# A linear-attention and SoLU kernel with the hidden features laid out eight to a partition: row-contiguous w_out, a permuting w_in cast, masks built first

## The chip, the cores and the metric

The kernel runs on one NeuronCore of a Trainium2 chip, in one launch. The metric is device time in microseconds (us). The kernel before was run ten times; the median is 157.78 us and the runs lie between 152.22 and 159.04 us. One further view comes from a profiled execution, whose own time is 158.03 us and whose span, from the first to the last instruction, is 156.3 us.

## What is computed

Two stages follow each other. The first is a linear attention with a decaying state per head (4 batches, 8 heads, 768 steps, head size 48):

```
for t in range(S):
    cur = einsum('bhd,bhe->bhde', u * k_t, v_t)
    y_t = einsum('bhd,bhde->bhe', r_t, state + cur)
    state = w_t[..., None] * state + einsum('bhd,bhe->bhde', k_t, v_t)
```

The result is seen as a matrix x of 3072 tokens by 384 features and goes through a feed-forward layer with 1024 hidden features:

```
h = x @ w_in                        # 384 -> 1024
solu = h * softmax(h)
ln = (solu - mean) / sqrt(var + 1e-6) * g_ln
out = ln @ w_out                    # 1024 -> 384
```

The sums over the 1024 hidden features (softmax, mean, variance, the last product) do not depend on the order in which the features are numbered, as long as w_in's columns, g_ln and w_out's rows use the same order.

## The kernel before

**Units.** The work is cut into 24 units: 6 chunks of 128 time steps by 4 batches. Each unit loads its k, r, w and v by four DMAs (192 KB each, in runs of one head of 48 floats, 192 bytes), all issued from SyncE's queue (SP). For each unit ScalarE takes the logarithm of w (`lw`), TensorE sums it along time (`cum`), ScalarE exponentiates (`exp`), VectorE scales k and r (`kp`), TensorE transposes them (`kt`, with `ident`), multiplies them to scores (`M`), applies them (`Y`), updates the state (`S`), and transposes the result (`X`). Then follow the hidden layer (`H`, 24 matmuls against `win_sb`), its exponential on ScalarE (`e`), the product (`he`) and the square (`hq`), the output product (`Oa`, `Ob`, against `w2`), the normalisation (`sq`, `qm`, `lv`), the scaled copy `o`, and the store `sto`.

**Order.** The order of all steps is written out by hand in the string `ORDER` (lines 24 to 54). A word names a stage, a unit and sometimes an engine (a for ScalarE, v for VectorE, g for GpSimd): `win2a` is the cast of slice 2 of w_in on ScalarE. The class `InOrder` (lines 57 to 75) chains the instructions that are made through `pe`, `act`, `dve`, `pool` and `sp`, so that each engine and the SP queue keep that order. Instructions made through `nc.gpsimd` or `nc.vector` directly, such as the memsets at the start, stand outside of the chain. The profile gives most instructions the line of `InOrder` (L71, or L68 for the first on an engine), so they are told apart by the names of their tiles.

**Weights.** The order on SP is: loads of units 0 to 2 with `small` (u and g_ln) among them, then `ldwin2`, `ldwin1`, `ldv1`, `ldwin0`, `ldwout0`, `ldwout1`, and the further loads. `ldwin` brings one slice of 128 rows of w_in (512 KB, 128 runs of 4 KB). `ldwout` brings four of the eight 128-row blocks of w_out (768 KB, 512 runs of 1.5 KB): hidden feature f sits on partition f % 128, block f // 128. The steps on the loaded weights are:

- `setup_rows` (line 200): TensorE spreads u over the partitions, then transposes the 8 x 128 tile `g_rows` into PSUM (`gt_ps`) with the 8 x 8 identity `ident_f`. `setup_rows_copy` (line 207): VectorE copies u to `u_bc` and makes the row scale `gr` from `gt_ps`.
- `setup_w_in` (line 222): ScalarE casts each slice of w_in to bf16, `win_f` to `win_sb`, three instructions.
- `setup_gain` (line 226): eight instructions `gw` scale w_out's blocks by `gr`; four run on ScalarE, two on VectorE, two on GpSimd. Blocks 0 to 3 come from the first half, 4 to 7 from the second.
- `setup_mean`, `setup_mean_copy`, `setup_w2` (lines 232 to 242): TensorE makes the column means from all eight `gw`, ScalarE copies them, and GpSimd adds them to each block, giving `w2`.

On ScalarE the order is `win2a win1a vb1a win0a gw1a gw0a e0 gw5a gw7a e1 lw3`. On TensorE it is `X1 H0 H1` and later `mean`; `H0` needs all three slices of `win_sb`.

**Masks.** `uti_neg`, `uts` and `ident` are 128 x 128 bf16 constants made on GpSimd (lines 153 to 162), and `ident_f` is made at line 192. `make_identity` is a library helper (a memset and an affine select, shown as masks.py in the profile).

Of the kernel before, what the change touches and what calls it, by code (L numbers as in the profile page):

```python
# [9 lines left out]
F32 = mybir.dt.float32  # L10
# [7 lines left out]
ALU = mybir.AluOpType  # L18
MULT, ADD = ALU.mult, ALU.add
# [59 lines left out]
def kernel(  # L79
# [12 lines left out]
    nc = tc.nc  # L92
    B, H, S, D = r.shape
    C = 128
# [5 lines left out]
    KF = DF // 128  # L100
    RDF = float(DF) ** 0.5
# [3 lines left out]
    pe, act, dve, pool, sp = (InOrder(tc, e) for e in (nc.tensor, nc.scalar, nc.vector, nc.gpsimd, nc.sync))  # L105
# [3 lines left out]
    consts = ctx.enter_context(tc.tile_pool(name="consts", bufs=1))  # L109
# [3 lines left out]
    small = ctx.enter_context(tc.tile_pool(name="small", bufs=4, space=bass.MemoryType.PSUM))  # L113

    live = [dict() for _ in units]
# [16 lines left out]


    u_row = consts.tile([1, DM], F32)
    g_rows = consts.tile([KF, 128], F32)
    win_f = consts.tile([128, KM, DF], F32)
    win_v = moe_w_in.rearrange("(ko ki) f -> ki ko f", ki=128)
    wout_f = consts.tile([128, KF, DM], F32)
    wout_v = moe_w_out.rearrange("(ko ki) d -> ki ko d", ki=128)

    def load_small():
        sp.dma_start(out=u_row, in_=u.rearrange("(o h) d -> o (h d)", o=1))
        sp.dma_start(out=g_rows, in_=moe_g_ln.rearrange("(ko ki) -> ko ki", ki=128))

    def load_w_in(j):
        sp.dma_start(out=win_f[:, j, :], in_=win_v[:, j, :])
# [1 line left out]
    def load_w_out(half):  # L148
# [2 lines left out]


    uti_neg = consts.tile([C, C], BF16)
    nc.gpsimd.memset(uti_neg, -1.0)
    nc.gpsimd.affine_select(out=uti_neg, in_=uti_neg, compare_op=ALU.is_ge, fill=0.0, base=0,
                            pattern=[[1, C]], channel_multiplier=-1)
    uts = consts.tile([C, C], BF16)
    nc.gpsimd.memset(uts, 1.0)
    nc.gpsimd.affine_select(out=uts, in_=uts, compare_op=ALU.is_gt, fill=0.0, base=0,
                            pattern=[[1, C]], channel_multiplier=-1)  # L160
    ident = consts.tile([C, C], BF16)
    make_identity(nc, ident)
    one_col = consts.tile([C, 1], BF16)
    nc.vector.memset(one_col, 1.0)
    own = consts.tile([C, HP, 2], F32)
# [18 lines left out]
    win_sb = consts.tile([128, KM, DF], BF16)  # L184
# [3 lines left out]
    nc.vector.memset(mean_w, -1.0 / DF)  # L188
    nc.vector.memset(w2[:, :, DM:], 1.0 / RDF)

    ident_f = consts.tile([KF, KF], F32)
    make_identity(nc, ident_f)
    ones_row = consts.tile([1, C], F32)
    nc.vector.memset(ones_row, 1.0)
    u_bc = consts.tile([C, H, D], BF16)
    gr = consts.tile([128, KF], F32)
# [3 lines left out]
    def setup_rows():  # L200
        u_ps = small.tile([C, DM], F32, tag="s", name="u_ps")
        pe.matmul(u_ps, lhsT=ones_row, rhs=u_row, start=True, stop=True)
        g_ps = small.tile([128, KF], F32, tag="s", name="gt_ps")
        pe.transpose(g_ps, g_rows, ident_f)
        live[0]["u_ps"], live[0]["g_ps"] = u_ps, g_ps

    def setup_rows_copy():
        dve.tensor_copy(out=u_bc.rearrange("t h d -> t (h d)"), in_=live[0]["u_ps"])
        dve.tensor_scalar(out=gr, in0=live[0]["g_ps"], scalar1=RDF, scalar2=None, op0=MULT)

    def copy(engine, out, in_):
        if engine is act:
            act.copy(out=out, in_=in_)
        else:
            engine.tensor_copy(out=out, in_=in_)
# [4 lines left out]
        pe.matmul(w_ps, lhsT=uti_neg, rhs=warm, start=True, stop=True)  # L220

    def setup_w_in(j, engine):
        copy(engine, win_sb[:, j, :], win_f[:, j, :])


    def setup_gain(f, engine):
# [359 lines left out]
    def part(stage, j):  # L586
# [5 lines left out]
        m=scores_copy, sel=scores_mask, Y=attend, y=y_copy, X=x_transposed, xT=x_copy, S=state, st=state_update,  # L592
        H=hidden, e=hidden_exp, he=hidden_mul, hq=hidden_square, Oa=part(output, 0), Ob=part(output, 1), sq=sums, qm=centre,
        lv=scale, o=scaled_out, sto=store, Oc=part(output, 2), oz=lambda i, engine: scaled_out(i, engine, 1),
        stz=lambda i: store(i, 1), sd=state_old, sa=state_add, win=setup_w_in, gw=setup_gain, wt=setup_w2, dm=warm_up,
        ldw=load("w", w), ldk=load("k", k), ldr=load("r", r), ldv=load("v", v), ldwin=load_w_in, ldwout=load_w_out,
    )
    once = dict(small=load_small, rows=setup_rows, ubc=setup_rows_copy, mean=setup_mean, mean_sb=setup_mean_copy)
    engines = dict(a=act, v=dve, g=pool)
    for word in ORDER.split():  # L600
        name, i, choice = re.fullmatch(r"([A-Za-z_]+)(\d*):?([a-z]?)", word).groups()
# [38 lines left out]
```

The softmax here doesn't subtract the row's maximum and nothing guards it: scores larger than these inputs give would overflow.

## Time and profile before

| what | value |
|---|---|
| median of ten runs | 157.78 us (152.22 to 159.04) |
| profiled execution: time, span | 158.03 us, 156.3 us |
| busy: TensorE, VectorE, GpSimd, ScalarE | 140.7, 130.2, 122.9, 119.9 us |
| DMA: read and written | 22.03 MB, 4.72 MB, 171 GB/s over the span |
| DMA packets, of these under 512 B | 104970, 100329 |
| w_in slice (512 KB): issue to landing | 5.5 us median of three |
| w_out half (768 KB): issue to landing | 7.3 and 9.9 us |
| cast of a w_in slice on ScalarE | 1046 ns, three of them |
| mean granted TensorE clock | 0.945 |

How to read it: a row of the timeline gives start, duration, engine, line, operation, the tiles written and read, and in brackets the idle time of that engine just before the row and what ended it. The chain of waits follows the instruction that ended last back to what released it, step by step. The granted clock is the share of TensorE's full speed that the throttle allowed. A row of the windows gives, for a stretch of time, the stretch's length and each engine's busy time (with its number of instructions), then the granted clock, the share of time in which the 16 DMA engines were busy, and the rate in GB/s.

### The profile page before, as it was taken

The page shows a single profiled execution, that of the slowest core. Times are in us where ns is not written, and L with a number is a line of the kernel's source. Part 1 is how long each engine was busy: PE and PEld are TensorE (multiplying, and loading weights), DVE is VectorE, ACT ScalarE, POOL GpSimd, SP SyncE. Part 2 cuts the span into 40 slices and gives each one's busy share as a digit, 9 for nine tenths or more (in the row PEclk, how much of TensorE's full clock was granted, in tenths as well). Part 3 has the DMA queues.
Part 4 walks back from the last instruction along what each step waited for, and adds up shares of the span by engine and source line. Part 5 has one row for each costly group of instructions (what it writes and reads, how often), then busy time and mean ns, then how long its engine had stood idle before and what let it go on. Part 6 is the DMA issues. An engine that isn't in the chain of part 4 may idle for free.

```text
span 156.3 us, 5293 instructions
## 1 busy us (share of the span) xinstructions
PE 140.7 (90%) x2154; PEld 110.1 (70%) x2156; DVE 130.2 (83%) x231; ACT 119.9 (77%) x232; POOL 122.9 (79%) x152
## 2 busy tenths in 40 slices
PE   6576796799999999999999899669999999999993
PEld 2255483577796787887788787546888688889771
DVE  7547939898997998979977989996889999998671
ACT  4356858888898979778989888555899888895742
POOL 3365975999889899999849999973799898976810
PEclk9955699689999999999999999977999999999999
DMA  5998998999979998989999799998988111011013
GB/s 99 193 199 285 379 303 163 204 198 202 207 166 192 210 216 170 216 161 202 209 193 223 160 236 202 219 257 163 270 171 192 55 50 55 2 55 55 12 64 130
DMA packets 104970, 27.09 MB, mean 173 GB/s; under 512 B 100329, under 2 KB 104562, under 8 KB 104946
## 3 DMA queue, kind: packets, MB, share of 16 engines
q1 hardware_dynamic: 104946, 26.75, 75.7%
q8 instruction: 17, 0.28, 0.7%
q14 instruction: 7, 0.06, 0.1%
HBM read 22.03 MB, written 4.72 MB: 171 GB/s over the span
## 4 chain that ended last, share of the span: by engine, by line
PE 43%; DMA 18%; DVE 14%; SPq 9%; ACT 8%; issue 4%; POOL 2%; POOLq 0%; DVEq 0%
PE o_ps L71 15%; PE h_ps L71 11%; SPq L71 9%; DMA kr_in<-in_k_dram 6%; DMA wout_f<-in_moe_w_out_dram 6%; DMA w_in<-in_w_dram 6%; PE kr_ps L71 4%; PE cum_ps L71 4%; PE m_ps L71 3%; DVE hq L71 3%; DVE kp L71 2%; PE y_ps L71 2%; DVE he L71 2%; PE s_ps L71 2%; ACT e L71 2%
## 5 line engine op out<-in xcount | busy, mean ns | idle before, releaser
L71 PE MATMUL o_ps<-w,he 128*128 128x385 bf16 (+2 forms) x200 | 43.6, 322 | 0.3 <-ACT sq L71 0.3
L71 PE MATMUL h_ps<-xT,win_sb 128*128 128x128 bf16 x576 | 35.9, 219 | 0.1
L71 PEld LDWEIGHTS <-win_sb 128*128 128x128 bf16 x576 | 32.8, 98 | 0.8 <-issue 0.2
L71 DVE TENSOR_TENSOR he<-h_ps,e 128x1024 bf16<-128x1024 f32 x24 | 29.2, 1216 | 2.7 <-ACT e L71 2.7
L71 PE MATMUL o_ps<-inv_col,e 128*128 128x1 bf16 x192 | 31.4, 167 | 0.0
L71 POOL TENSOR_TENSOR hq<-he 128x1024 bf16<-128x1024 bf16 x14 | 26.5, 1897 | 3.7 <-DVE he L71 2.4
L71 ACT ACTIVATE e<-h_ps 128x1024 bf16<-128x1024 f32 x24 | 24.5, 1022 | 5.8 <-PE h_ps L71 5.7
L71 PEld LDWEIGHTS <-he 128*128 128x128 bf16 x208 | 20.1, 98 | 11.3 <-issue 1.5
L71 ACT ACTIVATE cum_ps<-cum_ps 128x772 f32<-128x772 f32 (+1 forms) x24 | 19.2, 801 | 9.3 <-PE cum_ps L71 8.1
L71 DVE TENSOR_TENSOR kp<-cum_ps,kr_in 128x768 bf16<-128x768 f32 x24 | 22.8, 948 | 0.2 <-ACT cum_ps L71 0.2
L71 POOL TENSOR_TENSOR p<-kr_in 128x384 bf16<-128x384 f32 x18 | 18.4, 1029 | 4.7 <-DMA kr_in<-in_k_dram 4.7
L71 POOL TENSOR_TENSOR q<-p,u_bc 128x384 bf16<-128x384 bf16 x23 | 21.6, 943 | 0.6 <-DVE p L71 0.5
L71 POOL TENSOR_TENSOR dv<-vb,dg 128x384 bf16<-128x384 bf16 x22 | 18.2, 832 | 3.5 <-ACT vb L71 1.7
L71 PEld LDWEIGHTS <-kp 128*128 128x128 bf16 x272 | 17.9, 103 | 4.2 <-DVE kp L71 1.9
L71 DVE TENSOR_TENSOR m<-m_ps,uts 128x1024 bf16<-128x1024 f32 x14 | 17.0, 1222 | 3.3 <-PE m_ps L71 3.2
L71 PEld LDWEIGHTS <-e 128*128 128x128 bf16 x192 | 18.4, 96 | 0.1
L71 PE MATMUL kr_ps<-ident,kp 128*128 128x128 bf16 x192 | 16.1, 232 | 1.7 <-DVE kp L71 1.7
L71 ACT ACTIVATE lw<-w_in 128x384 bf16<-128x384 f32 x23 | 11.8, 523 | 3.3 <-DMA w_in<-in_w_dram 3.3
L71 POOL TENSOR_SCALAR_AFFINE_SELECT m<-m 128x1024 bf16<-128x1024 bf16 x10 | 11.0, 1102 | 3.7 <-ACT m L71 3.6
L71 PEld LDWEIGHTS <-kr 64*128 64x128 bf16 (+1 forms) x272 | 10.5, 98 | 4.5 <-DVE kr L71 2.0
L71 ACT COPY kr<-kr_ps 128x1024 bf16<-128x1024 bf16 x13 | 13.2, 1014 | 0.7 <-PE kr_ps L71 0.7
L71 PE MATMUL cum_ps<-lw,uti_neg 128*128 128x384 bf16 x24 | 8.5, 355 | 4.7 <-DVE kp L71 3.2
(93 smaller groups left out, 283.9 us busy)
## 6 DMA issues: line engine op xcount, KB each, us to landing
w_in<-in_w_dram SPq DMA_DIRECT2D x24, 192.0 KB, 3.9
kr_in<-in_r_dram SPq DMA_DIRECT2D x24, 192.0 KB, 3.7
kr_in<-in_k_dram SPq DMA_DIRECT2D x24, 192.0 KB, 4.1
v_in<-in_v_dram SPq DMA_DIRECT2D x24, 192.0 KB, 4.1
out_dram<-o SPq DMA_DIRECT2D x23, 192.0 KB, 2.8
win_f<-in_moe_w_in_dram SPq DMA_DIRECT2D x3, 512.0 KB, 5.5
wout_f<-in_moe_w_out_dram SPq DMA_DIRECT2D x2, 768.0 KB, 8.6
out_dram<-o SPq DMA_DIRECT2D x2, 96.0 KB, 1.6
```

The lines of the kernel that those rows point to most:

```text
L71: made = make(*args, **kwargs)
```

## The change

Hidden feature f goes to partition f // 8, slot f % 8, in place of partition f % 128, block f // 128. The edits:

```
-    g_rows = consts.tile([KF, 128], F32)
+    g_cols = consts.tile([128, KF], F32)
-    wout_v = moe_w_out.rearrange("(ko ki) d -> ki ko d", ki=128)
+    wout_v = moe_w_out.rearrange("(ki ko) d -> ki ko d", ki=128)
-        sp.dma_start(out=g_rows, in_=moe_g_ln.rearrange("(ko ki) -> ko ki", ki=128))
+        sp.dma_start(out=g_cols, in_=moe_g_ln.rearrange("(ki ko) -> ki ko", ki=128))
...
-    nc.gpsimd.memset(uti_neg, -1.0)
-    nc.gpsimd.affine_select(out=uti_neg, ...)
-    nc.gpsimd.memset(uts, 1.0)
-    nc.gpsimd.affine_select(out=uts, ...)
-    make_identity(nc, ident)
+    for t, value, keep, fill in ((uti_neg, -1.0, ALU.is_ge, 0.0), (uts, 1.0, ALU.is_gt, 0.0),
+                                 (ident, 0.0, ALU.not_equal, 1.0)):
+        pool.memset(t, value)
+        pool.affine_select(out=t, in_=t, compare_op=keep, fill=fill, base=0,
+                           pattern=[[1, t.shape[1]]], channel_multiplier=-1)
...
-    ident_f = consts.tile([KF, KF], F32)
-    make_identity(nc, ident_f)
...
-        g_ps = small.tile([128, KF], F32, tag="s", name="gt_ps")
-        pe.transpose(g_ps, g_rows, ident_f)
...
-        dve.tensor_scalar(out=gr, in0=live[0]["g_ps"], scalar1=RDF, scalar2=None, op0=MULT)
+        dve.tensor_scalar(out=gr, in0=g_cols, scalar1=RDF, scalar2=None, op0=MULT)
...
-        copy(engine, win_sb[:, j, :], win_f[:, j, :])
+        copy(engine, win_sb[:, j, :].rearrange("k (f m) -> k f m", f=KF), win_f[:, j, :].rearrange("k (m f) -> k f m", f=KF))
```

Each half of w_out is then 128 runs of 6 KB. g_ln comes as 128 runs of 32 bytes straight into the layout of `gr`. The cast of a w_in slice reads every eighth float (a step of 32 bytes) and writes contiguously. The three mask tiles are made through `pool`, so they stand in GpSimd's chain ahead of its first `p`. `ORDER` is the same.

More of the change, by code (lines that the diff above doesn't have):

```diff
@@ L153 @@
     uti_neg = consts.tile([C, C], BF16)
-    nc.gpsimd.memset(uti_neg, -1.0)
-    nc.gpsimd.affine_select(out=uti_neg, in_=uti_neg, compare_op=ALU.is_ge, fill=0.0, base=0,
-                            pattern=[[1, C]], channel_multiplier=-1)
     uts = consts.tile([C, C], BF16)
-    nc.gpsimd.memset(uts, 1.0)
-    nc.gpsimd.affine_select(out=uts, in_=uts, compare_op=ALU.is_gt, fill=0.0, base=0,
-                            pattern=[[1, C]], channel_multiplier=-1)
     ident = consts.tile([C, C], BF16)
-    make_identity(nc, ident)
+    for t, value, keep, fill in ((uti_neg, -1.0, ALU.is_ge, 0.0), (uts, 1.0, ALU.is_gt, 0.0),
[3 more added lines that the diff above has]
+                           pattern=[[1, t.shape[1]]], channel_multiplier=-1)
     one_col = consts.tile([C, 1], BF16)
@@ L202, in setup_rows @@
         pe.matmul(u_ps, lhsT=ones_row, rhs=u_row, start=True, stop=True)
-        g_ps = small.tile([128, KF], F32, tag="s", name="gt_ps")
-        pe.transpose(g_ps, g_rows, ident_f)
-        live[0]["u_ps"], live[0]["g_ps"] = u_ps, g_ps
+        live[0]["u_ps"] = u_ps
     def setup_rows_copy():
         dve.tensor_copy(out=u_bc.rearrange("t h d -> t (h d)"), in_=live[0]["u_ps"])
-        dve.tensor_scalar(out=gr, in0=live[0]["g_ps"], scalar1=RDF, scalar2=None, op0=MULT)
+        dve.tensor_scalar(out=gr, in0=g_cols, scalar1=RDF, scalar2=None, op0=MULT)
     def copy(engine, out, in_):
```

## The prediction

> **What bounds the kernel now.** I read the page first: its share of busy time, its forty slices, then the chain of waits, then the timeline of the first 30 us, where everything that the change touches runs.
>
> ```profile
> PE 140.7 (90%) x2154; PEld 110.1 (70%) x2156; DVE 130.2 (83%) x231; ACT 119.9 (77%) x232; POOL 122.9 (79%) x152
> PEclk9955699689999999999999999977999999999999
> DMA  5998998999979998989999799998988111011013
> ```
>
> TensorE is dense from about 30 us to the end, and DMA is dense until about 121 us (slice 31). Until about 24 us TensorE has gaps while DMA has none to speak of: the start is set by the arrival of data. The chain says which:
>
> ```profile
> 13.35 0.45 SPq L71
> 13.85 9.90 DMA wout_f<-in_moe_w_out_dram
> 23.78 1.12 ACT gw L71 x2
> 24.90 0.81 ACT e L71
> 25.71 0.52 ACT lw L71
> 26.27 0.58 PE cum_ps L71 x6
> ...
> 97.92 4.03 DVE hq L71
> 101.95 0.88 DVE kp L71
> 102.87 0.58 PE cum_ps L71 x6
> ```
>
> Up to 23.78 us the path is SP's queue and then the second half of w_out; after it ScalarE's queue in order. Later come stretches of TensorE, loads of k and w (up to 5 us each) and one odd piece, a square on VectorE of 4.03 us. The timeline rows of the steps that the change edits:
>
> ```profile
> 7.51 0.22 PE L71 MATMUL gt_ps<-ident_f,g_rows 8*128 8x8 f32 x1 [1.64 <-POOL ident_f masks.py:199]
> 15.31 1.05 ACT L71 CAST win_sb<-win_f 128x1024 bf16<-128x1024 f32 x1
> 16.53 1.05 ACT L71 CAST win_sb<-win_f 128x1024 bf16<-128x1024 f32 x1 [0.17 <-DMA win_f<-in_moe_w_in_dram]
> 18.58 1.04 ACT L71 CAST win_sb<-win_f 128x1024 bf16<-128x1024 f32 x1 [0.59 <-DMA win_f<-in_moe_w_in_dram]
> 20.67 1.12 ACT L71 ACTIVATE gw<-wout_f,gr 128x384 bf16<-128x384 f32 x2 [1.05 <-DMA wout_f<-in_moe_w_out_dram]
> 23.78 1.12 ACT L71 ACTIVATE gw<-wout_f,gr 128x384 bf16<-128x384 f32 x2 [1.07 <-DMA wout_f<-in_moe_w_out_dram]
> ```
>
> ScalarE waits for data before most of them, so it has slack to lose. The DMA columns of one-microsecond windows (last two: busy share, GB/s) price the transfers:
>
> ```profile
> 20.00:21.00 1.00, 1.00 (x21) 1.00 (x20) 0.95 (x3) 0.33 (x1) 0.26 (x1) 1.00 1.10 393
> 23.00:24.00 1.00, 1.00 (x6) 0.57 (x6) 0.22 (x1) 0.22 (x1) 0.21 (x1) 1.00 0.34 71
> 24.00:25.00 1.00, 0.96 (x6) 0.35 (x5) 1.00 (x3) 1.00 (x3) 0.00 (x0) 1.00 0.60 113
> 104.00:105.00 1.00, 1.00 (x16) 0.66 (x13) 0.99 (x4) 1.00 (x2) 0.51 (x1) 0.50 0.92 200
> ```
>
> The weights already move at about 390 GB/s in 1.5 KB and 4 KB runs; the unit loads in 192-byte runs make about 200. After the weights, DMA falls to 0.34 and 0.60 for 2 us: a part of w_out finishes late while the next loads are stuck behind it.
>
> [...] The new cast reads with a 32-byte step[...]. No row of the trace before has such a read. [...] the square at 97.84 us lasts 4.11 us, its median is 0.69, and GpSimd runs four instructions without a gap from 97.78 to 101.40.
>
> **The change part by part.** Sums are made on the profiled execution, 158.03 us (span 156.3 and 1.7 around it); that is 0.25 above the median shown.
>
> *Masks and transpose.* TensorE loses `gt_ps` and the wait for `ident_f`. `cum` of unit 1 began at 7.66; its input, the logarithm at 6.74 for 0.52, was there at 7.26, and the first such pair (3.58 + 0.52, matmul at 4.15) shows 0.05 between, so it can begin at 7.31: 0.35 us sooner. Behind it on TensorE the transposes at 8.10 and VectorE's copy at 8.97 gain the same. Then the cover comes: ScalarE waits for w of unit 2 until 9.76 (0.68 idle) and for v until 13.99 (0.69 idle), both data. So nothing of it arrives at 23.78; 0.35 is what it would be worth without that cover. GpSimd makes the same three memsets and selects (0.20 and 0.29 each) less 0.09 and 0.18 for `ident_f`; its first `p` waits for k until 6.07, which hides them. `gr` on VectorE now waits for g_ln's DMA instead of TensorE; issued at 2.55, it has until about 8.8 before it delays the copy at 8.97 behind it, and loads of 192 KB land in about 4 us. Zero.
>
> *g_ln's load.* 128 runs in place of 8, 7.5 more per DMA engine. A unit load has 1024 packets, 64 per engine, and 196.6 KB at 200 GB/s is 0.98 us, or 15 ns per packet: at most 0.11 us for everything behind it. SP's own issue rises from 0.29 to at most 0.42 (that of 1024 runs), hidden behind busy engines (0.97 to 1.00 from 2 to 8 us).
>
> *w_out.* Bytes are the same; packets fall from 1024 to 256, 48 fewer per engine. Of a small packet's 15 ns, 192 B at 24.4 GB/s per engine (390/16) explain 7.9, so about 7 ns are overhead: 48 x 7 = 0.34 us for both halves. The tail (1.1 us of DMA time lost between 23 and 25, from 0.66 + 0.40) may shrink, if it comes from many short runs, or stay. Bounds for the landing at 23.75: 0.1 later (all lost but g_ln's cost) to 1.4 - 0.1 = 1.3 earlier. I take 0.6 - 0.1 = 0.5 earlier: 23.25.
>
> *The cast.* 384 elements take 0.51 and 1024 take 1.046, so 0.84 ns per element and 0.19 fixed. Low bound: no penalty, 1.05. My value[...]: twice the element time, 1.91. High bound: four times, 3.6. At 1.91, in ScalarE's order: `win2a` 15.31 to 17.22; `win1a` to 19.1; `vb1a` 0.4; `win0a` 19.5 to 21.4. `H0` began at 19.93, so it now begins at 21.4 and ends at 22.8 (1.42 each). `gw1a gw0a` 21.4 to 22.5; `e0` 22.8 to 23.8 in place of 21.70 to 22.70; `gw5a gw7a` 23.8 to 24.9; `e1` from 24.8, as before. So the doubled cast just fits into the 1.05 and 1.07 us that ScalarE idled, and takes what the earlier w_out would have given there. With no penalty `e1` would come 0.5 sooner. What stays gained in either case is the DMA stream: the loads behind w_out (v of unit 2, for which GpSimd idled 1.95 until 25.16, k of unit 3, whose issue was held 4.02) run 0.5 sooner.
>
> *Sum.* 0 (masks) + 0 (g_ln's issue) + 0 (cast, hidden) - 0.5 to -0.6 for the loads on which the stretch up to 121 us feeds: 158.03 - 0.6 = 157.4, and by the 0.25 to the median 157.2 us. That is no change that can be told.
>
> **Rivals.** *The lock is avoided.* The 4.11 us square costs 4.11 - 0.69 = 3.4 us, and TensorE, idle 2.73 before 102.87, then runs at clock 0.50 for about 3.4 us, at half pace a loss of up to 1.7. It depends on which of two engines comes first within 0.06 us (97.78 and 97.84). A start shifted by 0.5 us may end it: 158.0 - 0.6 - 5.1 = 152.3. For it: ten runs of one code spread from 152.22 to 159.04, so about that much hangs on such timing. Against: both engines are released by the same order of work, and the median itself is at 157.78, so most runs seem to pay it.
>
> *The cast decides (slower).* The three casts stand ahead of `H0`. Above 1.91 us each, every 0.1 us more is 0.3 us at `H0`, `e0`, `e1` and `lw3`, with nothing left to hide it. At 3.0 us each it costs 3.3 us, beyond 2%; at the upper bound 3.6, 5.1 us, and I take 161.5, since idle TensorE also falls to half clock. [...]
>
> *The change in w_out's runs does nothing*[...]: the cast takes up the slack, g_ln costs 0.1, 158.0.
>
> **How the numbers follow.** Forecast 157.2, chance 0.40, own range 155.0 to 159.3 (1.3 for the w_out bound, 1 for scatter of the median among the ten times). No effect, 158.0: 0.08. Lock avoided, 152.3: 0.32. Cast, 161.5: 0.20. A difference of 2%, 3.2 us, is about what a measurement of this kernel can tell from none. Faster: 0.32 and 0.02 from the edge of the forecast, 0.34. Within 2%: 0.36 + 0.08 = 0.44. Slower: 0.20 + 0.02 = 0.22. The range reaches over the middle of both outer cases, 152.0 to 161.5; below and above it are left about a third of each, 0.1 + 0.1.
>
> **What the new profile would show.** Right: `gt_ps` and masks.py gone, first `cum` of unit 1 at 7.3; `win_sb` casts near 1.9 us; `gw` on ScalarE released at about 23.3 by w_out, `e1` at 24.8 or a little before; the windows after it busier than 0.34. Wrong: casts above 3 us and `H0` after 24 us (the slower rival); `gw` released at 23.8 as before (no effect); no VectorE square above 1 us and clock 1.00 around 104 us (the lock rival); a time outside of 155 to 159 with none of these.

## The result and the profile after

The changed kernel has a median of 154.18 us (152.92 to 158.96, 14 runs) beside 155.42 us of the kernel before (151.49 to 160.85, 51 runs). The ratio of the two is 1.0077, 95% interval 1.0043 to 1.0111: 0.8% slower, about 1.2 us. In 30 of those 51 executions of the kernel before and in 4 of 15 of the changed kernel (with the profiled one) the program takes about 4 to 5 us longer, which moves the medians; the ratio compares the executions without that. On another chip the changed kernel came to 1.0113 (1.0072 to 1.0153). The forecast was 157.2 us with a gain of 0.6 us. The time lies below its own range of 155.0 to 159.3 us, though inside the wide one of 152.0 to 161.5, and against the kernel before the sign is wrong: a small loss in place of a small gain.

The profiled execution of the changed kernel took 153.66 us with a span of 151.9 us; that of the kernel before took 158.03 us and held the 4.11 us square on VectorE, so the spans are not compared, but the first 30 us are. ScalarE's rows of the timeline after (start, duration, what; in brackets the idle time before and its end):

```profile
14.76 4.01 ACT L71 CAST win_sb<-win_f 128x1024 bf16<-128x1024 f32 x2
18.67 0.51 ACT L71 CAST vb<-v_in 128x384 bf16<-128x384 f32 x1
19.08 2.04 ACT L71 CAST win_sb<-win_f 128x1024 bf16<-128x1024 f32 x1
21.03 1.12 ACT L71 ACTIVATE gw<-wout_f,gr 128x384 bf16<-128x384 f32 x2
23.96 1.02 ACT L71 ACTIVATE e<-h_ps 128x1024 bf16<-128x1024 f32 x1 [1.81 <-PE h_ps L71]
24.88 1.11 ACT L71 ACTIVATE gw<-wout_f,gr 128x384 bf16<-128x384 f32 x2
26.26 1.02 ACT L71 ACTIVATE e<-h_ps 128x1024 bf16<-128x1024 f32 x1 [0.28 <-PE h_ps L71]
```

Two of ScalarE's rows before, the cast of v of unit 1 and the second exponential:

```profile
17.48 0.51 ACT L71 CAST vb<-v_in 128x384 bf16<-128x384 f32 x1
24.80 1.00 ACT L71 ACTIVATE e<-h_ps 128x1024 bf16<-128x1024 f32 x1
```

None of the rows after waits for a DMA any more. The casts take 2.04 us instead of 1.05; the second exponential starts at 26.26 us, before at 24.80. Three of TensorE's rows after, and the hidden layers before:

```profile
7.38 0.32 PE L71 MATMUL cum_ps<-lw,uti_neg 128*128 128x384 bf16 x1 [1.37 <-ACT lw L71]
19.23 0.48 PE L71 MATMUL y_ps<-vb,m 128*128 128x48 bf16 x8 [1.60 <-ACT vb L71]
21.18 5.04 PE L71 MATMUL h_ps<-xT,win_sb 128*128 128x128 bf16 x48 [0.19 <-ACT win_sb L71]
```

```profile
19.93 2.84 PE L71 MATMUL h_ps<-xT,win_sb 128*128 128x128 bf16 x48
```

Two windows after, and the first of them before (columns: stretch and its length, busy time with count of TensorE's matmuls, its weight loads, VectorE, ScalarE and GpSimd, then granted clock, DMA share and GB/s):

```profile
18.00:19.00 1.00, 0.00 (x0) 0.00 (x0) 0.00 (x0) 1.00 (x2) 0.85 (x2) 0.50 1.02 424
22.00:23.00 1.00, 1.00 (x13) 1.00 (x11) 0.76 (x3) 0.15 (x1) 0.37 (x1) 0.50 0.61 119
```

```profile
18.00:19.00 1.00, 0.99 (x14) 0.63 (x12) 0.95 (x2) 0.42 (x1) 0.92 (x2) 0.71 1.06 391
```

From 18 to 19 us neither TensorE nor VectorE has any work after the change (zeros for matmuls, weight loads and VectorE), while ScalarE casts: the cast of v of unit 1, 0.51 us, stands behind the two doubled casts, and unit 1's attention waits for it. TensorE's clock has been at 0.50 since 9 us in both executions. Before, it comes back in just this second (0.71) and is 1.00 from 19 us on; after the change it stays at 0.50 until 25 us, so the two hidden layers take 5.04 us instead of 2.84. This execution is the worst of its kind with casts of this length: in four others with the doubled casts (experiments below) TensorE waits 0.83 to 0.85 us for that cast of v instead of 1.60, and the two layers take 3.89 to 4.83 us. The DMA column shows the other side: 424 GB/s with 6 KB runs, before 391. The chain after, in order of time, goes through the casts where the chain before had w_out:

```profile
14.86 3.91 ACT win_sb L71 x2
...
19.18 1.96 ACT win_sb L71
...
21.18 5.04 PE h_ps L71 x48
...
26.45 0.59 PE w_ps L71 x2
27.04 1.30 PE mean_ps L71 x8
```

### The profile page after: what moved, and what is told of

Read it like the earlier page. It is cut to its first block, busy times and chain, and to the rows that moved or that the text cites. A ratio compares the mean times of both kernels' runs of the same rounds, so it can differ in the third digit from the quotient of the medians.

```text
span 151.9 us, 5288 instructions
## 1 busy us (share of the span) xinstructions
PE 139.4 (92%) x2153; PEld 110.7 (73%) x2155; DVE 127.2 (84%) x231; ACT 122.3 (80%) x232; POOL 122.6 (81%) x150
## 4 chain that ended last, share of the span: by engine, by line
PE 77%; ACT 7%; SPq 5%; DVE 5%; DMA 3%; issue 1%
PE o_ps L71 26%; PE h_ps L71 22%; PE kr_ps L71 6%; PE y_ps L71 5%; PE cum_ps L71 5%; SPq L71 5%; PE m_ps L71 4%; PE s_ps L71 4%; ACT win_sb L71 4%; DMA v_in<-in_v_dram 3%; PE x_ps L71 3%; DVE p L71 2%; DVE kp L71 1%; PE mean_ps L71 1%; PE w_ps L71 1%
## 5 line engine op out<-in xcount | busy, mean ns | idle before, releaser
L71 PE MATMUL o_ps<-w,he 128*128 128x385 bf16 (+2 forms) x200 | 42.2, 315 | 0.3 <-ACT sq L71 0.3
L71 PE MATMUL h_ps<-xT,win_sb 128*128 128x128 bf16 x576 | 38.1, 226 | 0.3 <-ACT win_sb L71 0.2
L71 PEld LDWEIGHTS <-win_sb 128*128 128x128 bf16 x576 | 35.0, 102 | 1.3 <-ACT win_sb L71 0.5
L71 ACT ACTIVATE e<-h_ps 128x1024 bf16<-128x1024 f32 x24 | 24.6, 1024 | 8.2 <-PE h_ps L71 8.1
L71 POOL TENSOR_TENSOR p<-kr_in 128x384 bf16<-128x384 f32 x19 | 19.7, 1043 | 5.6 <-DMA kr_in<-in_k_dram 5.6
L71 PEld LDWEIGHTS <-kp 128*128 128x128 bf16 x272 | 17.3, 100 | 4.5 <-DVE kp L71 2.5
L71 PE MATMUL kr_ps<-ident,kp 128*128 128x128 bf16 x192 | 15.5, 227 | 2.1 <-DVE kp L71 2.1
L71 PE MATMUL m_ps<-kr 64*128 64x128 bf16 x192 | 10.2, 229 | 1.3 <-DVE kr L71 1.3
```

The lines of the kernel that those rows point to most:

```text
L71: made = make(*args, **kwargs)
```

## The experiments

"Ratio" is to the kernel before on the same chip, with its 95% interval.

**1. Undo and do apart.** Four kernels: the permuting cast alone in the kernel before; the changed kernel with the plain cast; the masks alone; the changed kernel with more warm-up.

```
cast alone, in the kernel before:
-        copy(engine, win_sb[:, j, :], win_f[:, j, :])
+        copy(engine, win_sb[:, j, :].rearrange("k (f m) -> k f m", f=KF), win_f[:, j, :].rearrange("k (m f) -> k f m", f=KF))
plain cast, in the changed kernel: the same two lines the other way
masks alone, in the kernel before: the loop over the mask tiles, ident_f as a fourth in it
warm-up, in the changed kernel:
-        pe.matmul(w_ps, lhsT=uti_neg, rhs=warm, start=True, stop=True)
+        for _ in range(5 if i == 4 else 1):
+            pe.matmul(w_ps, lhsT=uti_neg, rhs=warm, start=True, stop=True)
```

> The kernel before with the permuting cast alone (w_out, g_ln and the masks as before; the hidden features of w_in are then in another order than those of w_out, so the output is another function). Theory 'cast': the three casts take 2.04 us instead of 1.05 as in the changed kernel, and as nothing else changes, the hidden layer of unit 0 starts at about 21.5 us instead of 19.9, TensorE stays at half clock through it, the second exponential starts at 26 to 27 us instead of 24.8; ratio to the kernel before 1.008 to 1.015. Rival 'later': the cast is hidden in the waits for w_out, the loss of the changed kernel comes from elsewhere; ratio 1.000 within 0.3%.

Measured: 1.0107 (1.0076 to 1.0138), casts of 2.0 us, hidden layer from 21.43 us, second exponential at 25.96. The two hidden layers took 3.89 us, between the 2.84 us at a granted clock of 1.00 (kernel before) and the 5.04 us at 0.50 for all but the last microsecond (changed kernel). By these lengths TensorE ran at half pace for a part of them and not all through; that is an estimate, as the clock column of this profile reads 1.00 from 16 to 26 us. The cast alone costs what the whole change costs, or more.

> The changed kernel with the contiguous cast of before (features of w_in and w_out in different orders, so the output is another function). Theory 'cast': casts at 1.05 us, hidden layer at about 19.4 us at full clock, second half of w_out landed at about 22.2 us, second exponential at about 23.3 us instead of 24.8 before and 26.3 changed; ratio 0.985 to 0.995. Rival 'later': ratio as in the changed kernel, 1.005 to 1.010.

Measured: 0.9976 (0.9955 to 0.9996). The loss is gone. The second half of w_out is there at 21.4 us, but the second exponential comes at 23.7, later than expected, and the gain is 0.4 us only, less than the 0.5% to 1.5% that were expected. As the place of the loss "cast" holds, and "later" falls.

> The kernel before with all masks and both identities made first in GpSimd's chain, nothing else. Theory 'cast': the sums of unit 1 begin at 7.3 us instead of 7.66, but the 0.35 us are gone at the next wait for data; ratio 1.000 within 0.3%. Rival 'phase': a shift of 0.35 us at the start moves the later phases and the whole time; ratio off by more than 0.5% in either direction.

Measured: 0.9998 (0.9973 to 1.0023). The masks are worth nothing, "phase" falls.

> The changed kernel with four more warm-up matmuls (into the same unread tile) where TensorE idles behind the cast of v, from 17.4 to 19.2 us. Theory 'clock' (most of the loss is the half clock in the first two hidden layers, 5.04 us where they took 2.84 before): clock 1.00 from about 20 us, the two hidden layers in about 2.9 us, second exponential at about 25.0 us instead of 26.3; ratio to the kernel before 0.997 to 1.001. Theory 'queue' (ScalarE's queue alone carries the delay): hidden layers shorter, but the time stays at 1.006 to 1.010.

Measured: 1.0024 (1.0000 to 1.0048). TensorE's and ScalarE's rows of this kernel:

```profile
16.88 1.98 PE L71 MATMUL w_ps<-warm,uti_neg 128*128 128x512 bf16 x5
20.35 2.85 PE L71 MATMUL h_ps<-xT,win_sb 128*128 128x128 bf16 x48 [0.31 <-ACT win_sb L71]
```

```profile
23.84 1.01 ACT L71 ACTIVATE e<-h_ps 128x1024 bf16<-128x1024 f32 x1
```

The casts are as slow as in the changed kernel, but the matmuls whose result nobody reads keep TensorE busy: its clock is 1.00 from 19 us on, and the hidden layers take 2.85 us. That brings back about two thirds of the loss or more (from 1.008 or 1.011 to 1.002, a little above what "clock" expected and well below what "queue" did). So the delay in ScalarE's queue costs mostly through TensorE's clock.

**2. What the cast pays for.** The same permutation with scattered writes; two or four neighbouring features per partition instead of eight; and the permutation moved to the weight loads.

```
scattered writes: "k (f m) -> k m f" on the output, win_f read in order
two or four neighbours (G = 2 or 4; the loads of w_out and g_ln follow the same order):
+    wout_v = moe_w_out.rearrange("(q ki r) d -> ki q (r d)", ki=128, r=G)
...
+        copy(engine, win_sb[:, j, :].rearrange("k (q r m) -> k q r m", r=G, m=128),
+             win_f[:, j, :].rearrange("k (q m r) -> k q r m", r=G, m=128))
weight loads: plain cast, and
+    lhsT=win_sb[:, j, :].rearrange("k (m f) -> k f m", f=KF)[:, f, :]
```

> The changed kernel with the same permutation in the cast, but the loops exchanged: floats are read contiguously and the bf16 results written with a step of 256 bytes. [...] cast 1.05 us, ratio to the kernel before 0.996 to 0.999, as with the plain cast. If scattered writes cost as well: cast 2 us or more, ratio 1.005 to 1.012.

Measured: 1.0648 (1.0594 to 1.0701), far more than either expectation (0.996 to 0.999 and 1.005 to 1.012).

> The changed kernel with two instead of eight neighbouring features on a partition: w_out comes in runs of 3 KB, g_ln in runs of 8 bytes, and the cast reads with a step of 8 bytes. Theory 'lines' [...]: cast 1.05 us, w_out still at 400 GB/s or more, ratio 0.996 to 0.999. Rival 'any step' (a cast that is not contiguous costs double): cast 2.04 us, ratio 1.005 to 1.010.

Measured: 0.9988 (0.9961 to 1.0016).

> The same with four neighbouring features: runs of 6 KB as in the changed kernel, a step of 16 bytes. Theory 'lines': [...] cast 2.04 us as at 32 bytes, ratio 1.005 to 1.010. Rival 'the step grows the price': cast near 1.5 us, ratio 1.000 to 1.004.

Measured: 1.0103 (1.0034 to 1.0172).

The rows for the cast in these three, from the view of the tile `win_sb` (least, median and greatest duration in ns), first the scattered writes, then a step of 8 bytes, then of 16:

```profile
L71 ACT CAST win_sb<-win_f x3: 4742/4754/5043, 14.3 to 23.8; 128x1024 bf16<-128x1024 f32 x3
```

```profile
L71 ACT CAST win_sb<-win_f x3: 1117/1121/1123, 14.8 to 17.8; 128x1024 bf16<-128x1024 f32 x3
```

```profile
L71 ACT CAST win_sb<-win_f x3: 2025/2029/2049, 14.7 to 19.0; 128x1024 bf16<-128x1024 f32 x3
```

1046 ns contiguous, 1121 at 8 bytes, 2029 at 16, 2045 at 32: a step in the price between 8 and 16 bytes and almost none from there to 32. Those are the lengths that "lines" gave, but for 1121 ns in place of 1.05 us at 8 bytes; what makes the step was not shown. The factor on the elements comes to about two: 2045 against 1046 ns, each less 0.19 us that do not depend on the elements (an estimate from 0.51 us for 384 elements and 1046 ns for 1024). "Any step" and "the step grows the price" fall. The cast with scattered writes of bf16 takes more than twice as long as the one with scattered reads of floats (4754 against 2045 ns).

> The changed kernel with a contiguous cast; the permutation is made by TensorE's weight loads instead, which read every eighth bf16 (a step of 16 bytes), 576 of them. If the loads stay at 98 ns or stay hidden: ratio 0.996 to 0.999. If they double like ScalarE's read, 576 times about 0.1 us, of which a part is hidden behind the matmuls of 56 ns each: 10 to 50 us more, ratio 1.07 to 1.35.

Measured: 1.0144 (1.0103 to 1.0185), weight loads of 147 ns instead of 98. Neither: 576 times 49 ns is 28 us, but the time is only 2.2 us above the kernel before (2.5 above the kernel with the plain cast). Weight loads run beside matmuls: the page of the kernel before has 140.7 us of matmuls and 110.1 us of weight loads in a span of 156.3 us, so at least 94.5 us of them side by side. The rest of the 28 us is probably hidden there; how much is hidden was not measured.

**3. Another engine, and where the gain went.** With the plain cast the rest of the change was worth 0.4 us (0.1 to 0.7), with two neighbours 0.2 us with an interval that reaches over zero. The kernel of two neighbours also has longer runs of w_out, so it was the base for looking further. Together with it ran the middle cast on VectorE.

```
order moved (in the kernel of two neighbours, and in the kernel before):
-win0a dm6 X0 m2v dv1v ldwout0 ... dm2 X1 xT0v xT1v dg2 H0 H1
+win0a dm6 X0 m2v xT0v dv1v ldwout0 ... dm2 H0 X1 xT1v dg2 H1
middle cast on VectorE, in the changed kernel: win1a -> win1v
```

> The kernel of two features per partition with two words of the order moved: VectorE copies unit 0's transpose before it makes unit 1's attention term, and TensorE starts the hidden layer of unit 0 ahead of unit 1's transpose. Theory 'next limit' (w_out's earlier landing was worth little because the hidden layer of unit 0 waited for VectorE at 20.06 us): hidden layer at about 19.3 us, second exponential at about 23.0 us instead of 23.7, ratio to the kernel before 0.991 to 0.996. Rival 'no more to gain at the start': ratio as without the move, 0.997 to 1.001.

Measured: 1.0002 (0.9976 to 1.0028), second exponential at 23.16 us.

> The kernel before with the same two words moved. Theory 'next limit': ScalarE still waits for the second half of w_out, which lands at about 22.9 us as in the kernel before, so the second exponential stays at about 24 us; ratio 0.997 to 1.001. Rival 'order alone': the move is what helps; ratio as in the kernel with two features and this order.

Measured: 1.0023 (1.0000 to 1.0046), second exponential at 24.35 us. The hidden layer of unit 0 does start sooner with the moved order (in the first kernel 6.10 us behind the first cast of v instead of 6.60), and ScalarE then waits for the second half of w_out, 0.46 us in the first kernel and 1.46 in the second. But counted from the first cast of v the second exponential is not sooner (10.40 us, without the move 10.21; table below), and the time does not fall either: "next limit" falls for the first kernel.

> The changed kernel itself, beside the others on one chip: ratio 1.004 to 1.011 as measured before.

Measured: 1.0113 (1.0072 to 1.0153).

> The changed kernel with the middle of its three casts on VectorE instead of ScalarE. If VectorE pays for the step of 32 bytes as ScalarE does: about 2.1 us there, which stands ahead of its attention copy for unit 0; ScalarE is done 2 us sooner; ratio 1.000 to 1.008. If VectorE reads such steps at full pace (about 1.1 us): ratio 0.996 to 1.002.

Measured: 1.0041 (1.0018 to 1.0064). The cast took 1.60 us on VectorE, between the two expected lengths, and the second exponential came at 24.49.

The profiled execution of the kernel of two neighbours with the moved order happened to be one with the long square, with GpSimd's row and VectorE's:

```profile
95.34 0.91 POOL L71 TENSOR_TENSOR q<-p,u_bc 128x384 bf16<-128x384 bf16 x1
...
96.99 1.95 POOL L71 TENSOR_TENSOR p<-kr_in 128x384 bf16<-128x384 f32 x2
```

```profile
95.41 4.08 DVE L71 TENSOR_TENSOR hq<-he 128x1024 bf16<-128x1024 bf16 x1
```

It is the same unit as in the kernel before (97.84 us there): VectorE's square begins 0.07 us after GpSimd's `q` and ends at 99.49 us, 0.55 us behind the last of four GpSimd instructions in a row (98.94). In the kernel before it ends at 101.95, and the four of GpSimd at 101.40, 0.55 us apart as well. That the square waits for those four is a reading of these times. In the kernel of two neighbours without the moved order the square began at 94.67, GpSimd's next at 94.82, and it took 0.68.

**4. The loads.** Half of v's loads was taken away (an eighth of the units' bytes).

```
+            heads = slice(0, H // 2 if name == "v" else H)
+            sp.dma_start(out=L[name][:, heads], in_=src[b, heads, ...])
```

> The kernel before with only half of v loaded (heads 4 to 7 take the values of heads 0 to 3, so the output is another function): 12% fewer bytes for the units, otherwise the same work. The base for the next two. If the loads set the pace after the start: ratio to the kernel before 0.96 to 0.99. If TensorE's queue alone does: 0.995 to 1.0.

Measured: 0.9942 (0.9917 to 0.9966). Between the two expectations: 0.9 us.

> The kernel of two features and moved order, with the same half of v. Theory 'loads' (its 0.8 us at the start was worth nothing because the loads, not the start, end later): with lighter loads it is 0.4% or more below the kernel before with half of v. Rival 'start has slack' (an earlier start is lost in waits of the engines on each other): equal to it within 0.2%.

Measured: 0.9929 (0.9904 to 0.9954), 0.0013 below the base, where "loads" asked for 0.004 or more, with intervals that overlap widely. "Loads" falls.

> The changed kernel with the same half of v. Both theories: a late start is paid in full; 1.0% or more above the kernel before with half of v. If instead the loads were what made the late start cost, the distance shrinks below 0.5%.

Measured: 1.0073 (1.0049 to 1.0098), 1.3% above the base: the late start costs as much with lighter loads.

**5. The additions that make w2.** Their start on GpSimd went along with the time in most profiles so far, from 25.8 us (level) over 26.6 (1.004) and 28.0 (1.010) to 35.8 (1.065). Not all of them fit: it was 26.66 us in the kernel before itself, 28.94 in the first profile of the changed kernel (1.008) and 26.11 with the strided weight loads (1.014).

```
-wt2g ... wt3g
+wt2v ... wt3v
```

> The kernel of two features per partition (order otherwise as before) with two of the eight additions that make w2 moved from GpSimd to VectorE. Theory 'w2' (the path after the start goes through GpSimd's eight additions, 7.8 us from about 25.8 us, which w_out's earlier landing does not start sooner, as the column means stand behind the first two hidden layers on TensorE): GpSimd is free 1.9 us sooner, ratio to the kernel before 0.988 to 0.995. Rival 'only a mark' (the start of the additions goes with the time but nothing waits for them): 0.997 to 1.001, as without the move.

Measured: 1.0075 (1.0051 to 1.0099), slower.

> The kernel before with the same two additions on VectorE. Theory 'w2': the same gain, ratio 0.988 to 0.995, as the additions start at the same time in both. Rival 'only a mark': 0.998 to 1.002.

Measured: 1.0059 (1.0034 to 1.0085), slower as well. Both expectations missed. The gain of "w2" did not come, though in the first kernel GpSimd was done with its additions at 30.96 us instead of 33.57 and then waited itself. But the move brings a delay of its own, so what a free GpSimd alone is worth was not measured. On VectorE the additions stand ahead of the scaling `kp` of unit 3, and TensorE waits for that (rows of the first of the two kernels):

```profile
27.39 1.06 DVE L71 TENSOR_TENSOR w<-gw,mean_sb 128x384 bf16<-128x384 bf16 x1
28.37 0.94 DVE L71 TENSOR_TENSOR kp<-cum_ps,kr_in 128x768 bf16<-128x768 f32 x1
```

```profile
29.37 1.03 PE L71 MATMUL kr_ps<-ident,kp 128*128 128x128 bf16 x8 [1.38 <-DVE kp L71]
```

`kp` starts 0.51 us later than without the move (27.86), TensorE idles 1.38 us instead of 0.43, and the transposes then take 1.03 us instead of 0.62. In the kernel before the same eight took 1.05 us at 29.83 us, where the granted clock was 0.50.

**The start, measured in one way.** The arrival of the first loads differs by more than 1 us between executions. So here the start is taken from the first cast of v (ScalarE) to the second exponential, both from the timeline of the profiled execution. The kernels with half of v and the one with strided weight loads are left out; the two with moved additions lose their time only after this stretch.

| kernel | from, to (us) | lag | ratio |
|---|---|---|---|
| before, two additions on VectorE | 13.70, 23.72 | 10.02 | 1.0059 |
| two neighbours | 13.46, 23.67 | 10.21 | 0.9988 |
| changed, plain cast | 13.33, 23.71 | 10.38 | 0.9976 |
| two neighbours, order moved | 12.76, 23.16 | 10.40 | 1.0002 |
| two neighbours, two additions on VectorE | 12.85, 23.30 | 10.45 | 1.0075 |
| before | 13.99, 24.80 | 10.81 | 1 |
| masks alone | 12.90, 23.96 | 11.06 | 0.9998 |
| before, order moved | 13.17, 24.35 | 11.18 | 1.0023 |
| changed, warm-up | 12.58, 23.84 | 11.26 | 1.0024 |
| changed, one cast on VectorE | 12.91, 24.49 | 11.58 | 1.0041 |
| cast alone | 13.70, 25.96 | 12.26 | 1.0107 |
| four neighbours | 13.40, 25.80 | 12.40 | 1.0103 |
| changed (second chip) | 13.24, 25.69 | 12.45 | 1.0113 |
| changed (first chip) | 13.44, 26.26 | 12.82 | 1.0077 |
| changed, scattered writes | 12.94, 33.27 | 20.33 | 1.0648 |

The late starts, from 12.26 us on, stand clear of the rest. Against the kernel before, 1.6 us more cost 1.7 us (1.1% of 151.4), and 9.5 us more cost 9.8. The early ones do not. The kernel before with two additions moved has the same code as the kernel before up to its second exponential, with short casts and 1.5 KB runs, and its profile shows the earliest start of all; w_out was there without a wait:

```profile
22.71 1.11 ACT L71 ACTIVATE gw<-wout_f,gr 128x384 bf16<-128x384 f32 x2
23.72 1.01 ACT L71 ACTIVATE e<-h_ps 128x1024 bf16<-128x1024 f32 x1
```

So one code gives lags of 10.02 and 10.81 us, and the 10.21 to 10.45 us of the kernels with longer runs and short casts lie between them. That the longer runs of w_out make the start earlier is not shown by these profiles, each of which is one execution.

The exponentials of all 24 units show how a late start lasts: taken against the kernel with the masks alone, the second exponential of the changed kernel (second chip) comes 1.73 us later, the third 1.42, and from the seventh unit to the last the distance stays between 1.25 and 1.26 us. After about 57 us both executions run at one pace, and nothing makes up for the late start.

## Why the prediction was wrong

**The step that failed** is the one that the prediction puts as "`H0` began at 19.93, so it now begins at 21.4 and ends at 22.8 (1.42 each)", and with it "So the doubled cast just fits into the 1.05 and 1.07 us that ScalarE idled". The start was nearly right, 21.18 us. The duration was not: the two hidden layers took 5.04 us together instead of 2.84 (3.89 to 4.83 in the other executions with doubled casts). The prediction took their 1.42 us each from a trace in which TensorE had just come back to full clock. I followed what stands behind the casts on ScalarE and who waits for the last of them, but not who waits for the small cast of v among them. That one was late by 1.7 us (5.23 us behind the first cast of v instead of 3.49), TensorE had nothing to do for 1.60 us, its clock stayed at 0.50, and it ran the hidden layers at half pace. The second exponential came at 26.26, not 24.8. The warm-up kernel shows this part by itself: same casts, hidden layers at 2.85 us, ratio 1.0024.

Point by point:

- *The cast*: estimated 1.91 us, measured 2.04. The doubling was right and the size nearly so; why a step of 32 bytes doubles the cast was not shown. The slower rival had the right place but the wrong price. It counted ScalarE's queue alone, 0.3 us for every 0.1 us above 1.91, which at 2.04 makes 0.4 us, and it brought in half clock only at 3.6 us a cast. The loss was 1.2 to 1.7 us, most of it by half clock, at casts of 2.04.
- *w_out*: said to land at 23.25, came at 22.2 (issue at about 13.5, 8.7 us), 1.6 sooner than before instead of 0.5; 0.4 of that is an earlier issue. The tail after the weights stayed, with a DMA share of 0.61 from 22 to 23 us. That the longer runs do nothing for the rate, as one rival had it, is neither confirmed nor refuted. From 16 to 20 us the six profiles with 1.5 KB runs show 386 to 394 GB/s, the nine with 6 KB runs 388 to 430: 430 in the first profile of the changed kernel, 393 in the second. So up to a tenth more came with longer runs, and not in every execution. The landing of the second half scatters too, 9.0 to 10.6 us behind its issue with 1.5 KB runs and 8.6 to 10.8 with 6 KB runs.
- *Gain passed on*: the 0.5 us that the loads behind w_out were to gain did not show as such. With the cast made cheap the ratio lies between 0.9976 and 1.0002.
- *The level*: 157.2 us was built on an execution with the long square and on a median of ten, 157.78; 51 runs of the same kernel have 155.42. That the time came out 3 us below the forecast says nothing of the change.
- *Masks, transpose, g_ln*: zero, as said; 0.9998 for the masks. The sums of unit 1 began at 7.38 us, said was 7.3, and nothing of it arrived.
- *The lock*: the square's longest time in the profile after is 1.23 us and the clock from 104 to 106 us is 1.00, which the prediction had named as signs of that rival. But it is not the change that ends the long square: of the 19 profiles only two have it, the kernel before and the one of two neighbours with the moved order, at the same unit, and the kernel with the masks alone has none. Whether the change shifts how often the long one comes was not tested.

**What stays open** is whether the longer runs of w_out give an earlier start at all, and whether such a start would last. The gain with the plain cast, 0.4 us, is smaller than the scatter of the start between executions. Lighter loads did not bring it out, and what GpSimd's additions hold back was not measured alone. The stretch up to the seventh unit, from 25 to 57 us, adds differences of its own: two executions of the changed kernel lie 0.57 us apart at the second exponential and 0.92 from the seventh on.

## What to carry to other kernels

When an instruction in an engine's queue becomes longer, list everything behind it in that queue up to the next wait for data, the small instructions too, and ask of each who is idle until it comes. Idle time of TensorE can be paid twice: here it waited 1.60 us, and behind the wait the two hidden layers took 5.04 us, at a granted clock of 0.50 up to 25 us, instead of 2.84 at 1.00. Slack that is read off as "ScalarE waits for data here" covers ScalarE's own work only. If a layout asks for a permuting cast of floats on ScalarE, keep the read step at 8 bytes (1.12 us a cast here, against 2.03 at 16 bytes and 2.04 at 32): two neighbours per partition gave w_out runs of 3 KB and the time of the kernel before (0.9988), where four and eight cost 1% (1.0103, 1.0077 and 1.0113). And before a shift of half a microsecond in one profile is read as an effect, look at a second profile of the same code: here the unchanged start moved by 0.8 us.

## What the runs showed of the hardware

- ScalarE, 128 x 1024 floats to bf16: 1.05 us contiguous, 1.12 with a read step of 8 bytes, 2.03 at 16, 2.04 at 32; 4.75 with contiguous reads and bf16 writes 256 bytes apart. VectorE took 1.60 us at a read step of 32 bytes.
- TensorE's weight load of 128 x 128 bf16 from SBUF: 98 ns contiguous, 147 with a step of 16 bytes.
- DMA moved 386 to 394 GB/s from 16 to 20 us with w_out in 1.5 KB runs (six profiles), and 388 to 430 with w_out in 6 KB runs (nine profiles).
- VectorE's square `hq` took 4.11 us in the kernel before and 4.08 us in the kernel of two neighbours with the moved order. In both it began 0.06 to 0.07 us behind a GpSimd instruction and ended 0.55 us behind the fourth of a row of them. It took 0.68 us where it began 0.15 us ahead of GpSimd's next.
- TensorE's granted clock came back from 0.50 to 1.00 between 18 and 19 us in the kernel before and in the changed one with more warm-up, where no wait between 15 and 18 us was longer than 0.47 us, and only between 25 and 26 us in the changed kernel, where it waited 1.60 us up to 19.23.
- TensorE's slower pace also came behind waits shorter than 1.6 us, and no single length told it in these runs. The transposes of unit 3 took 1.03 us behind a wait of 1.38 us that followed one of 1.31 (two neighbours, two additions on VectorE), and 0.62 us in the kernel of two neighbours with the 1.31 and one of 0.43. In the kernel before the granted clock fell from 1.00 to 0.50 between 28 and 29 us, with no wait longer than 1.31 us since 20 us.
